# Weight conversion in the first chunk: steps of several pieces grouped by kind, and moved ahead of other work

## The chip, the cores and the metric

The kernel runs on one core of a Trainium2 chip. The core has a matrix engine (TensorE; PE in the profile), VectorE (DVE), ScalarE (ACT), GpSimd (POOL) and SyncE (SP), which here only issues transfers. Each engine works through its instructions in their order, and waits on semaphores for what others make. The metric is the device time of one execution in microseconds (us); less is better.

## The reference, cut to what matters

```python
# q, k, v, o_gate: (4, 8, 768, 40); i_gate, f_gate: (4, 8, 768)
for t in range(S):                                  # an mLSTM cell
    m_new = np.maximum(f_gate[:, :, t] + m, i_gate[:, :, t])
    f_stab = np.exp(f_gate[:, :, t] + m - m_new)
    i_stab = np.exp(i_gate[:, :, t] - m_new)
    C = f_stab * C + i_stab * einsum('bhd,bhe->bhde', vt, kt)
    n = f_stab * n + i_stab * kt
    y[:, :, t] = sigmoid(o_gate) * (C @ qt) / max(abs(n @ qt), 1)
x = y.transpose(0, 2, 1, 3).reshape(3072, 320)
h = x @ w_in                                        # w_in: (320, 2048)
out = (h * np.cos(h)) @ w_out                       # w_out: (2048, 320)
```

The two weights are float64 on the host: `randn(...)` times a float64 scale. They reach the chip as pairs of 32-bit words.

## The kernel before

The sequence is cut into 6 chunks of 128 steps; with 4 batches that makes 24 cells, numbered n = 4 c + b. The cells of chunk 0 are computed first, in a written order (`first_cells`). After that `both_parts(c, b)` (L956) does the feed-forward part of chunk c in two halves, f2 = 2b and 2b + 1, and along with it cell n = 4 (c + 1) + b of the next chunk. A half covers 256 of the 2048 columns of w_in. The change is in chunk c = 0 alone; "half 0" to "half 7" below are its f2 = 0 to 7, with cells 4 to 7.

The order of the program is the order on each engine (`tc.manual_schedule`). In a half come: `Up` (TensorE: w_in times x into two PSUM banks; L645 for the two 128-row parts, L639 for the last 64 rows, which come last in even halves and first in odd ones), `near` (ScalarE, L653), `rest` (VectorE, L656: the remainder), `sin` (ScalarE, L661) and `gate` (VectorE, L665), which frees the PSUM bank. There are two such banks, so `Up` of the next half waits for the gates of this one. `down_slot` multiplies what the half before gave with w_out (L677). In an even half the cell's scores (L479), their weighing (L485), its values (L505 to L514), `seam` (L597) and `normalize_turned` (from the transpose of the gate, oT, L457, to xT, L534) stand in between; in an odd half its state (L622), `weigh_k` of the next cell (GpSimd, kw, L407), the two transposes of its q and k (`turn_blocks`, VectorE, L452; the scores of the next half need them), and `scale_q` (GpSimd, qG, L461). `seam_out` in an odd half issues the transfer xL on ScalarE's queue.

**The conversion.** w_in comes in pieces `in f a`, `in f b` (128 rows by 512 columns each) and `in f c` (the last 64 rows, laid out as 128 by 256), f = 0 to 3; piece f holds the columns of halves 2f and 2f + 1. w_out comes in pieces `out0` to `out7` of 128 by 640; out p is used by `down` of half p. Each is brought as bits by SyncE (L139, four transfers of 128 KB for a and for b; L174, four of 64 KB for c; L180, one of 640 KB) and made float32 in six steps:

- `take_apart`: two on ScalarE, L150 (out of the high words) and L152 (low words, in place);
- `put_together`: a clamp (L157) and two shifts in one instruction (L159), both on VectorE with one input; a bitwise step on VectorE with two inputs (L161); an addition on GpSimd (L162).

The bits of w_in pieces lie in a ring of four buffers, those of w_out pieces in a ring of three. So the transfer of out p + 3 waits for the addition of out p, and on SyncE's queue everything behind it waits too. `next_out` (L952) converts the next w_out piece and issues the transfer of the one three later.

Before, in1a is converted in half 0, behind the cell's normalizing. Then:

| half | place: piece |
| --- | --- |
| 1 | before state and gates: in1b; after the gates: in1c; then SyncE: in2, q, k, v, E of cells 6 and 7; transposes, qG; out1, transfer of out4 |
| 2 | after the gates: in2a; out2, transfer of out5; behind normalizing: in2b |
| 3 | before state and gates: in2c; SyncE: in3, q, k, v, E, G of cells 8 and 9; transposes, qG; out3, transfer of out6 |
| 4 | after the gates: in3a; out4, transfer of out7; behind normalizing: in3b |
| 5 | before state and gates: in3c; transposes, qG; out5 |
| 6, 7 | after the gates: out6; after transposes and qG: out7 |

Of the kernel before, what the change touches and what calls it, by code (L numbers as in the profile page):

```python
# [11 lines left out]
FP = mybir.dt.float32  # L12
I32 = mybir.dt.int32
# [3 lines left out]
OP = mybir.AluOpType  # L17
# [12 lines left out]
def kernel(  # L30
# [20 lines left out]
    nc = tc.nc  # L51
# [87 lines left out]
            nc.sync.dma_start(out=bits[rows, 0:n], in_=piece)  # L139
        return bits  # L140

    def to_float32(dst, bits):
        take_apart(dst, bits)
        put_together(dst, bits)

    def take_apart(dst, bits):
        n = dst.shape[1]
# [3 lines left out]

        nc.scalar.activation(out=bits[:, 0:n, 0], in_=lo, func=AF.Copy, scale=2.0 ** -29)  # L152

    def put_together(dst, bits):
        n = dst.shape[1]
        hi, t, m = bits[:, 0:n, 1], dst.bitcast(I32), bits[:, 0:n, 0]
        nc.vector.tensor_scalar(out=t.bitcast(FP), in0=t.bitcast(FP), scalar1=LEAST, scalar2=GREATEST,  # L157
                                op0=OP.max, op1=OP.min)
        nc.vector.tensor_scalar(out=t, in0=t, scalar1=5, scalar2=2, op0=OP.logical_shift_left,  # L159
                                op1=OP.logical_shift_right)  # L160
        nc.vector.scalar_tensor_tensor(out=t, in0=hi, scalar=TOP2, in1=t, op0=OP.bitwise_and, op1=OP.bitwise_or)  # L161
        nc.gpsimd.tensor_tensor(out=t, in0=t, in1=m, op=OP.add)  # L162

# [665 lines left out]
    def first_cells():  # L829
        nc.vector.memset(nil, 0.0)  # L830
        gates_in()
        nc.scalar.copy(out=ident_b, in_=ident)
        load(0, "qk")
        later_gates_in()
        load(0, "v")
        load(1, "qk")
        load_o(0, (0, 1))
        load(1, "v")
        load(2, "qk")
        load_E(0)  # L840
# [60 lines left out]
        load_two(B, "Kv")  # L901
        load_E(B + 1)
        load_o(1)
        outs.append((0, weights_out(0)))
        weigh(2)
        decay_exponents(3)
        turn_out(3)
        seam_out(1)
        values(2)
        decay(3)  # L910
        weigh_k(3)
        state(1)
        normalize(2)
        scores(3)
        pg = gates_turn()
        warm(1)
        seam(2)
        weigh(3)
        to_float32(*pieces.pop(0))
        decay_exponents(B)  # L920
        pieces.extend(weights_in(1))
        outs.extend((p, weights_out(p)) for p in range(1, 3))
        seam_out(2)
        state(2)
        for piece in pieces[0:2]:
            take_apart(*piece)
        gates_keep(*pg)
        values(3)
        normalize(3)
        put_together(*pieces.pop(0))  # L930
        warm(3)
        seam(3)
        seam_out(3)
        put_together(*pieces.pop(0))
        low_dimensions(B)
        turn_blocks(B)
        state(3)
        load_E(B + 2)
        decay(B)
        sigmoid(1)  # L940
        weigh_k(B)
        odd_values(B)
        scale_q(B)
# [5 lines left out]

        nc.scalar.activation(out=spot, in_=spot, func=AF.Sin)  # L950

    def next_out():  # L952
        p, piece = outs.pop(0)
        to_float32(*piece)
        if p + 3 < NF // 2:
            outs.append((p + 3, weights_out(p + 3)))  # L956

    def both_parts(c, b):

        n = (c + 1) * B + b  # L960
        cell = n < N
        for i in range(2):
            f2 = 2 * b + i
            up = Up(c, f2)
            if cell and i == 0:
                scores(n)
                if c == 0 and b == 0:

                    warm(8, psum_o())
            if cell and i == 1:  # L970
                if n % 2 == 1 and n > B + 1 and n + 3 < N:
                    load_two(n + 3, "Kv")
            for e in range(2):
                up.near(e)
            for e in range(2):
                up.rest(e)
            if i == 0:
                if cell:
                    weigh(n)
                    if n + 1 < N:  # L980
                        decay_exponents(n + 1)
                    if n == B:
                        clear_low()
                for e in range(2):
                    up.sin(e)
                    up.gate(e)
                if c > 0:
                    sums(c, f2)
                if b == 0 and c == 1:
                    sigmoid(c + 1)  # L990

                if c == 0 and b > 0 and pieces:
                    to_float32(*pieces.pop(0))
                if c == 0:
                    next_out()
                if cell and n + 1 < N:
                    decay(n + 1)
            else:
                if cell:
                    seam_out(n)  # L1000
                if pieces:
                    to_float32(*pieces.pop(0))
                if cell:
                    state(n)
                for e in range(2):
                    up.sin(e)
                    up.gate(e)
                if c > 0:
                    sums(c, f2)
                if n == B + 1:  # L1010
                    low_dimensions(n + 1)
                while pieces:
                    to_float32(*pieces.pop(0))
                if cell and n + 1 < N:
                    weigh_k(n + 1)
                    odd_values(n + 1)
            if i == 1 and b == B - 1 and 0 < c < NC - 2:
                sigmoid(c + 2)
                sin_next()
            down_slot(c, f2)  # L1020
            if f2 == 0 and c > 1:
                for p in range(2):
                    combine_first(c - 1, p)
            if cell and i == 0:
                turn_gate(n)
                values(n)
                seam(n)
                normalize_turned(n)
                fade(n)
                if c == 1 and b < 3:  # L1030
                    weight_sums(b + 1)
                if n % 2 == 1 and n > B + 1 and n + 3 < N:
                    load_two(n + 3, "qk")
                if n > B + 1 and n + 3 < N:
                    load_E(n + 3)
                if b == B - 2 and c + 2 < NC:
                    load_o(c + 2)
                if c == 0 and pieces:
                    to_float32(*pieces.pop(0))
                sin_next()  # L1040
            if f2 == 0 and c > 1:
                for p in range(2):
                    combine(c - 1, p)
            if i == 1:
                if c == 0 and b + 2 < B:
                    pieces.extend(weights_in(b + 2))
                    load_two((n + 3) // 2 * 2)
                    load_E(n + 3)
                if cell and n + 1 < N:
                    turn_blocks(n + 1)  # L1050
                    scale_q(n + 1)
                if c == 0:
                    next_out()
                if (c, f2) == (0, LAST):
                    weight_sums(0)

    pieces, outs = [], []
# [41 lines left out]
```

## Time and profile before

| | us |
| --- | --- |
| median of 3 runs | 540.6 (539.52 to 541.74) |
| the profiled execution, its time | 540.66 |
| its span, first to last instruction | 538.9 |
| TensorE busy | 520.1 |
| VectorE busy | 421.9 |
| ScalarE busy | 285.7 |
| GpSimd busy | 224.7 |
| mean granted TensorE clock | 0.972 |

Half 1 begins at about 59 us, half 7 ends at about 140 us. How to read the profile's rows: in a timeline a row has the start in us, the duration, engine, line, operation, what is written and read, the count, and in brackets how long the engine stood idle before and what ended that. Matmuls of several instructions are merged into one row. A row of the chain has start, duration and what the end of the program waited for at that time; "DMA" is a transfer from its issue to its landing. "SPq" and "ACTq" are queues that issue transfers: their duration is that of issuing. A row of the waits has who waited for whom, the sum in us, the number and the longest. A row of one line has minimum, median and maximum duration in ns.

### The profile page before, as it was taken

Reading aid. Unit: us, or ns where it says so; the run is one execution under the profiler, and the core shown is the slowest. Engines: PE = TensorE matmul, PEld = TensorE weight load, DVE = VectorE, ACT = ScalarE, POOL = GpSimd, SP = SyncE. Lnnn points to the kernel's source line nnn. Section 1 sums busy time; section 2 is a strip of 40 time slices with the busy share of each in tenths; the row PEclk is TensorE's granted clock in tenths of the full one; section 3 lists DMA queues with packets and bytes.
Section 4 is the critical chain, followed back from the end, with each engine's and each line's share of the span. In section 5 each row is a group of like instructions: output and inputs, shape, how many; then the busy total and the mean of one; then the engine's idle time right before and its main releaser. Section 6 shows DMA issues by size and latency. Waiting matters only on the chain.

```text
span 538.9 us, 10497 instructions
## 1 busy us (share of the span) xinstructions
PE 520.1 (97%) x3844; PEld 353.7 (66%) x3844; DVE 421.9 (78%) x907; ACT 285.7 (53%) x546; POOL 224.7 (42%) x369
## 2 busy tenths in 40 slices
PE   7999879899999999999999999999999999999996
PEld 4885445545566767757767767767667767576755
DVE  5565889998788897898878898878898878663636
ACT  2587958666475446826527826526836522222221
POOL 7435454555477573533542632542421421221211
PEclk9587989999999999999999999999999999999999
DMA  9999884959847539329248329249220000000001
GB/s 137 220 213 233 248 169 142 213 92 253 176 116 171 67 94 191 42 93 202 28 120 174 43 88 193 35 125 174 40 79 7 2 5 6 19 33 1 0 1 49
DMA packets 99939, 57.81 MB, mean 107 GB/s; under 512 B 62304, under 2 KB 92608, under 8 KB 99888
## 3 DMA queue, kind: packets, MB, share of 16 engines
q1 hardware_dynamic: 96496, 55.64, 47.4%
q10 hardware_dynamic: 3248, 1.33, 1.2%
q8 instruction: 30, 0.49, 0.4%
q0 software_dynamic: 144, 0.18, 0.1%
q14 instruction: 21, 0.17, 0.1%
HBM read 51.71 MB, written 4.11 MB: 104 GB/s over the span
## 4 chain that ended last, share of the span: by engine, by line
PE 73%; DMA 9%; DVE 8%; SPq 4%; POOL 2%; ACT 1%; issue 1%; DVEq 0%; POOLq 0%
PE pup L645 26%; PE acc L755 24%; PE pup L639 8%; PE po L677 3%; PE late L755 3%; DMA bits<-in_moe_w_in_dram 3%; PE ps L479 3%; PE vt L514 2%; PE vt L505 2%; PE pu L597 1%; DMA E<-M_d 1%; DVE t L452 1%; DMA xL<-xT 1%; DMA bits<-in_moe_w_out_dram 1%; DMA G<-G_d 1%
## 5 line engine op out<-in xcount | busy, mean ns | idle before, releaser
L645 PE MATMUL pup<-xT,w_in_sb 128*128 128x512 f32 x384 | 177.8, 606 | 4.8 <-DVE g L665 4.5
L653 ACT ACTIVATE n<-pup 128x512 int32<-128x512 f32 x96 | 54.0, 595 | 195.3 <-PE pup L639 143.7
L645 PEld LDWEIGHTS pup<-xT,w_in_sb 128*128 128x128 f32 x384 | 70.6, 193 | 92.2 <-issue 87.9
L656 DVE SCALAR_TENSOR_TENSOR n<-pup,n 128x512 f32<-128x512 f32 x96 | 63.1, 687 | 76.3 <-ACT n L653 75.0
L719 POOL TENSOR_TENSOR D<-g 128x128 f32<-128x128 f32 x40 | 19.8, 495 | 218.6 <-DVE g L665 218.6
L661 ACT ACTIVATE n<-n 128x512 f32<-128x512 f32 x96 | 57.6, 627 | 21.8 <-DVE n L656 13.1
L665 DVE SCALAR_TENSOR_TENSOR g<-pup,n 128x512 f32<-128x512 f32 x96 | 61.7, 684 | 4.1 <-ACT n L661 3.5
L755 PE MATMUL acc<-w_out_sb,g 128*128 128x160 f32 x320 | 58.6, 304 | 0.0
L755 PE MATMUL acc<-T,g 128*128 128x160 f32 x320 | 58.0, 301 | 0.1
L639 PE MATMUL pup<-xL,w_in_l 64*128 64x512 f32 x192 | 54.2, 641 | 0.0
L755 PEld LDWEIGHTS acc<-w_out_sb,g 128*128 128x128 f32 x320 | 47.8, 190 | 5.6 <-issue 4.2
L755 PEld LDWEIGHTS acc<-T,g 128*128 128x128 f32 x320 | 48.1, 190 | 3.6 <-issue 2.9
L402 ACT ACTIVATE E<-E,tab 128x128 f32<-128x128 f32 x160 | 49.0, 388 | 0.3
L677 PE MATMUL po<-w_out_sb,g 128*128 128x320 f32 x128 | 36.2, 436 | 1.8 <-POOL w_out_sb L162 1.8
L755 PE MATMUL acc<-T,S 128*128 128x160 f32 x160 | 35.0, 301 | 0.0
L479 PEld LDWEIGHTS ps<-t,t 40*128 40x128 f32 x384 | 26.0, 196 | 11.3 <-issue 6.6
L677 PEld LDWEIGHTS po<-w_out_sb,g 128*128 128x128 f32 x128 | 24.1, 190 | 13.2 <-POOL w_out_sb L162 2.4
L485 DVE TENSOR_TENSOR E<-ps,E 128x512 f32<-128x512 f32 x48 | 30.7, 681 | 0.5 <-PE ps L479 0.5
L461 POOL TENSOR_TENSOR qG<-t,G 128x512 f32<-128x512 f32 x20 | 25.6, 1281 | 13.0 <-DVE t L452 6.5
L639 PEld LDWEIGHTS pup<-xL,w_in_l 64*128 64x128 f32 x192 | 14.5, 185 | 23.3 <-issue 19.0
L755 PE MATMUL acc<-w_out_sb,S 128*128 128x160 f32 x160 | 28.8, 299 | 0.0
L950 ACT ACT_TABLE_LOAD x22 | 28.2, 1283 | 0.4
(175 smaller groups left out, 883.5 us busy)
## 6 DMA issues: line engine op xcount, KB each, us to landing
E<-M_d SPq DMA_DIRECT2D x22, 512.0 KB
qr<-in_q_dram SPq DMA_DIRECT2D x36, 160.0 KB
kr<-in_k_dram SPq DMA_DIRECT2D x36, 160.0 KB
G<-G_d SPq DMA_DIRECT2D x20, 256.0 KB
bits<-in_moe_w_out_dram SPq DMA_DIRECT2D x8, 640.0 KB
bits<-in_moe_w_in_dram SPq DMA_DIRECT2D x32, 128.0 KB
out_dram<-o_sb SPq DMA_DIRECT2D x24, 160.0 KB
ks<-in_k_dram SPq DMA_DIRECT2D x10, 320.0 KB
```

The costliest lines, as they stand in the source:

```text
L402: nc.scalar.activation(out=Es[n][:, h], in_=Es[n][:, h], func=AF.Exp, scale=-1.0, bias=tab[:, c, 0, g:g + 1])
L479: nc.tensor.matmul(ps[j][:, p], kT[r, p], qT[r, p], start=True, stop=True)
L485: nc.vector.tensor_tensor(out=w, in0=pss[n][j], in1=w, op=OP.mult)
L639: nc.tensor.matmul(pu, w_in_l[r, f2], xL[c][r].rearrange("p b t -> p (b t)"), start=ahead, stop=not ahead)
L645: nc.tensor.matmul(pu.rearrange("p (b t) -> p b t", b=B), w_in_sb[:, i, ts(2 * f2 + e, 128)], xT[c][:, i:NK * B:NK], start=(i == 0 and not ...
L653: nc.scalar.activation(out=self.n[e], in_=self.pu[e], func=AF.Copy, bias=0.25)
L656: nc.vector.scalar_tensor_tensor(out=self.n[e].bitcast(FP), in0=self.pu[e], scalar=0.25, in1=self.n[e], op0=OP.add, op1=OP.subtract)
L661: nc.scalar.activation(out=r, in_=r, func=AF.Sin, scale=TWO_PI_DOWN)
L665: nc.vector.scalar_tensor_tensor(out=g, in0=self.pu[e], scalar=TWO_PI, in1=self.n[e].bitcast(FP), op0=OP.mult, op1=OP.mult)
L677: nc.tensor.matmul(po[c][b], gs[c, f][:, ts(b, C)], w_out_sb[:, f], start=(f == 0), stop=(f == NF - 1))
L755: nc.tensor.matmul(a, lhs, rhs, start=start, stop=stop)
L950: nc.scalar.activation(out=spot, in_=spot, func=AF.Sin)
```

## The change

`to_float32` takes several pieces: ScalarE's steps of all of them, then the clamps and shifts of all (`bound`, new), then the bitwise steps and additions of all. `next_out` takes the w_in pieces that are converted together with its own. In odd halves of chunk 0 all of them stand behind the gates and ahead of `down_slot`, the transfers of SyncE and the transposes. `weigh_k` goes behind `scale_q` in chunk 0. After it:

| half | place: pieces |
| --- | --- |
| 1 | after state and gates: in1b, in1c, out1 together, transfer of out4; then SyncE: in2, q, k, v, E; transposes, qG, kw |
| 2 | after the gates: in2a, out2 together, transfer of out5; behind normalizing: in2b |
| 3 | after state and gates: in2c, out3 together, transfer of out6; SyncE: in3, q, k, v, E, G; transposes, qG, kw |
| 4 | after the gates: in3a, out4 together, transfer of out7; behind normalizing: in3b |
| 5 | after state and gates: in3c, out5 together; transposes, qG, kw |
| 6, 7 | after the gates: out6; out7 |

In `first_cells` the order of instructions stays as it was.

```diff
-    def to_float32(dst, bits):
-        take_apart(dst, bits)
-        put_together(dst, bits)
+    def to_float32(*made):
+        for dst, bits in made:
+            take_apart(dst, bits)
+        for dst, bits in made:
+            bound(dst)
+        for dst, bits in made:
+            put_together(dst, bits)
...
+    def bound(dst):
+        t = dst.bitcast(I32)
+        nc.vector.tensor_scalar(out=dst, in0=dst, scalar1=LEAST, scalar2=GREATEST, op0=OP.max, op1=OP.min)
+        nc.vector.tensor_scalar(out=t, in0=t, scalar1=5, scalar2=2, op0=OP.logical_shift_left,
+                                op1=OP.logical_shift_right)
+
     def put_together(dst, bits):
         n = dst.shape[1]
         hi, t, m = bits[:, 0:n, 1], dst.bitcast(I32), bits[:, 0:n, 0]
-        nc.vector.tensor_scalar(out=t.bitcast(FP), in0=t.bitcast(FP), scalar1=LEAST, scalar2=GREATEST,
-                                op0=OP.max, op1=OP.min)
-        nc.vector.tensor_scalar(out=t, in0=t, scalar1=5, scalar2=2, op0=OP.logical_shift_left,
-                                op1=OP.logical_shift_right)
...
-    def next_out():
+    def next_out(*made):
         p, piece = outs.pop(0)
-        to_float32(*piece)
+        to_float32(*made, piece)
         if p + 3 < NF // 2:
             outs.append((p + 3, weights_out(p + 3)))
...
-                if c == 0 and b > 0 and pieces:
-                    to_float32(*pieces.pop(0))
                 if c == 0:
-                    next_out()
+                    next_out(*[pieces.pop(0) for _ in range(min(b, len(pieces), 1))])
...
                 if cell:
                     seam_out(n)
-                if pieces:
-                    to_float32(*pieces.pop(0))
                 if cell:
                     state(n)
...
                 if n == B + 1:
                     low_dimensions(n + 1)
-                while pieces:
-                    to_float32(*pieces.pop(0))
+                if c == 0:
+                    next_out(*pieces)
+                    pieces.clear()
                 if cell and n + 1 < N:
-                    weigh_k(n + 1)
+                    if c > 0:
+                        weigh_k(n + 1)
                     odd_values(n + 1)
...
                 if cell and n + 1 < N:
                     turn_blocks(n + 1)
                     scale_q(n + 1)
-                if c == 0:
-                    next_out()
+                    if c == 0:
+                        weigh_k(n + 1)
```

More of the change, by code (lines that the diff above doesn't have):

```diff
@@ L918, in first_cells @@
         weigh(3)
-        to_float32(*pieces.pop(0))
+        to_float32(pieces.pop(0))
         decay_exponents(B)
@@ L929, in first_cells @@
         normalize(3)
+        bound(pieces[0][0])
         put_together(*pieces.pop(0))
@@ L933, in first_cells @@
         seam_out(3)
+        bound(pieces[0][0])
         put_together(*pieces.pop(0))
@@ L1011, in both_parts @@
                     low_dimensions(n + 1)
-                while pieces:
-                    to_float32(*pieces.pop(0))
+                if c == 0:
+                    next_out(*pieces)
+                    pieces.clear()
                 if cell and n + 1 < N:
-                    weigh_k(n + 1)
+                    if c > 0:
+                        weigh_k(n + 1)
                     odd_values(n + 1)
@@ L1038, in both_parts @@
                 if c == 0 and pieces:
-                    to_float32(*pieces.pop(0))
+                    to_float32(pieces.pop(0))
                 sin_next()
```

## The prediction

> **What bounds the kernel now.** I read the page first, then the waits of TensorE, then the timelines of each engine from 60 to 145 us, then the chain over the same stretch. TensorE is busy 520.1 of 538.9 us. From 145 us on nothing that this change touches makes it wait, so what the first chunk gains or loses there goes to the end one for one.
>
> ```profile
> PE 520.1 (97%) x3844; PEld 353.7 (66%) x3844; DVE 421.9 (78%) x907; ACT 285.7 (53%) x546; POOL 224.7 (42%) x369
> PE pup L645 <- DVE g L665: 4.5, 3, 2.4
> PE po L677 <- POOL w_out_sb L162: 1.8, 3, 0.7
> 70.71 5.37 PE L645 MATMUL pup<-xT,w_in_sb 128*128 128x512 f32 x8 [2.41 <-DVE g L665]
> 95.40 3.67 PE L645 MATMUL pup<-xT,w_in_sb 128*128 128x512 f32 x8 [1.19 <-DVE g L665]
> 118.37 3.67 PE L645 MATMUL pup<-xT,w_in_sb 128*128 128x512 f32 x8 [0.94 <-DVE g L665]
> ...
> 74.45 1.44 DVE L159 TENSOR_SCALAR w_out_sb<-w_out_sb 128x640 int32<-128x640 int32 x1
> 83.50 1.48 DVE L159 TENSOR_SCALAR w_out_sb<-w_out_sb 128x640 int32<-128x640 int32 x1
> 83.20 1.43 POOL L162 TENSOR_TENSOR w_in_sb<-w_in_sb,bits 128x512 int32<-128x512 int32 x1 [3.72 <-ACT bits L152]
> ```
>
> Read there: TensorE waits three times for the gates of halves 1, 3 and 5 (2.41, 1.19, 0.94 us) and three times, 1.8 us together, for out1, out3 and out5. The second shift of a w_out piece lasts 0.49 us alone and 1.44 to 1.48 us when GpSimd adds at that moment. The second set of rows is SyncE's queue and the chain.
>
> ```profile
> 62.71 8.50 SPq L139 DMA_DIRECT2D bits<-in_moe_w_in_dram  x8
> 71.31 2.63 SPq L174 DMA_DIRECT2D bits<-in_moe_w_in_dram  x4
> ...
> 91.71 0.37 SPq L180 DMA_DIRECT2D bits<-in_moe_w_out_dram  x1
> 92.34 4.02 DMA bits<-in_moe_w_in_dram
> 97.10 4.56 DMA bits<-in_moe_w_in_dram
> 105.38 0.68 DVE w_in_sb L161
> 124.68 4.58 PE po L677 x16
> ...
> 398.57 0.58 DVE L714 TENSOR_TENSOR S<-g 128x128 f32<-128x128 f32 x1
> 398.55 0.46 POOL L719 TENSOR_TENSOR D<-g 128x128 f32<-128x128 f32 x1 [8.82 <-DVE g L665]
> 378.30 0.29 DVE L714 TENSOR_TENSOR S<-g 128x128 f32<-128x128 f32 x1
> L534 DVE TENSOR_TENSOR xT<-yt,db x20: 557/559/1010, 63.9 to 452.7; 128x384 f32<-128x384 f32 x20
> ```
>
> The pieces in2 are issued from 62.71 to 73.94, in3 from 92.34 to 99.32. Their use begins on ScalarE at 79.72 (in2a) and 102.71 (in3a).
>
> **What the change gains.** In halves 1, 3 and 5 one w_in conversion leaves the place ahead of the gates: in1b is 1.52 us of VectorE (67.46 to 68.98), in2c and in3c 1.25 each. Gates move up by as much, and so does TensorE's next Up, as far as the three waits go: at most 2.41 + 1.19 + 0.94 = 4.5 us. out1, out3, out5 come ahead of the two transposes: at most 1.8 us. The clamps and shifts no longer meet an addition: about 1 us of VectorE in each of halves 1, 2 and 4 and 0.7 in each of 3 and 5 (two clamps at 0.55 and 0.93 for 0.28 and 0.49); VectorE has no idle time from 100.85 to 122.9. After the 2.41 us hole the granted clock was 0.5 from 72.1 to 75.5, so another 1.7 us (5.37 less 3.67) could come back. The ceiling is 4.5 + 1.8 + 1.7 = 8.0 us.
>
> **What it costs, half by half.** All durations are start-to-start in the timelines: clamp and shift 0.45 + 0.46 us for in a/b, 0.32 + 0.33 for in c, 0.53 + 0.53 for out; bitwise steps (L161) 0.61, 0.34, 0.74; additions (L162) 1.28, 0.70, 1.55; ScalarE's two steps 0.58, 0.34, 0.69 each; 0.12 us from engine to engine.
>
> Half 1. State and gates now follow the remainders (67.5): 0.88 + 1.2 us, first gate done at 69.0, TensorE starts Up of half 2 at 69.1. But in1b and in1c are weights of this very Up. in1b's bitwise step now stands behind six clamps and shifts: 69.6 + 2.62 = 72.2, done at 72.85, its addition (which before ended at 70.5) at 74.4. TensorE has 1.82 us of work without it (to 70.95) and then waits 3.6 us. From 74.55: 1.82 + 1.06 + scores 0.9 = 78.35, or 80.05 if one stretch of 3.4 us falls to half clock as after the 2.41 us hole. Before, that point was 78.04, and the next matmuls began at 78.50. So half 1 gives back all it won: -0.15 to +1.5.
>
> SyncE. out4's transfer is now issued ahead of in2, q, k, v and E. It writes the buffer of out1, so it waits for out1's addition, and the whole queue with it. Additions: in1b 73.15 to 74.45, in1c, out1 to 77.45 (the order of steps is below). So in2 is issued from 77.5, not from 62.71. How long until in2a is there: from out5's issue at 91.71 the first slab of in3a landed at 96.36 (4.65 us, 0.79 MB) and the second slab of in3c, issued at 97.10, at 101.66 (9.95 us, 1.83 MB). Between them out plus a whole "a" piece (1.18 MB) takes 6.6 us; I take 6.5, with 4.3 (the first slab's own 4.02 and 0.3) and 7.4 (the chain's 5.36 us for out0 at 44.65, and four slabs at 0.5) as bounds. in2a lands at 84.0. ScalarE comes to it at 81.8 and waits; behind it stand out2's steps, the decay of the next cell and in2b; on VectorE the clamps wait, and normalizing the cell behind them. Clamps of in2a at 84.8, of out2 at 86.1, the oT transpose at 88.5 (before 85.76), remainders of half 3 at 94.1 (before 91.21), first gate of half 3 at 96.85, Up of half 4 at 97.0 against 95.40: the step won is spent, +1.5.
>
> Half 3. in2c's clamps wait for ScalarE, which copies q and k (1.68 us) first; out3's clamps go ahead of in2c's bitwise step; its addition ends at 102.0 where TensorE wants it at 100.6 (97.0 + 3.63): 1.5 us. Third set of matmuls of w_out at 104.3 against 101.72: +2.5.
>
> SyncE again. out6 goes ahead of in3 and waits for out3's addition, which ends at 103.6. in3a lands at 110.2, 7 us after ScalarE needed it before (102.71) and 4.5 after it is ready now. VectorE stands 3.3 us. oT at 114.6 (before 108.75), remainders of half 5 at 120.2 (114.18); the gates no longer wait for in3c: 122.3 (117.53); Up of half 6 at 123.1 (118.37); w_out's fifth set at 129.2 against 124.68: **+4.5**. From there TensorE runs on as before; in halves 6 and 7 out6 and out7 have 1.5 us and more of slack on VectorE (idle 1.68 at 135.94), and GpSimd's sums begin after out7 and qG as before.
>
> **Two-input steps beside additions.** The trace says what meets whom: L714 (both inputs in SBUF) lasts 0.29 us alone and 0.58 beside GpSimd's L719; L534 goes from 0.56 to 1.01 us. So in the groups a bitwise step and an addition take turns, and that is in the times above: out1's bitwise step waits for in1b's addition (0.85 to 1.3 us), in2c's and in3c's additions wait for out3's and out5's bitwise step (0.65). Without the taking of turns the same working ends at 2.6 instead of 4.5; I keep 4.5 because the rows show it. [...]
>
> On GpSimd out1's, out3's and out5's additions now stand ahead of qG, and kw behind it: qG of cell 5 runs from 77.5 to 78.7 and is wanted at 84.4, kw (1.0 us) later still; nothing, as long as w_out's matmuls (4.4 us) lie between.
>
> **Sum.** The profiled execution took 540.66 us with a span of 538.9, as good as the median 540.6. 540.66 + 4.5 = 545.2 us. With a landing in 4.3 us the same working gives +0.5 to +1.4, with 7.4 us +6.5 us.
>
> **Rivals.**
> 1. The transfers aren't late (in2 and in3 come by the time ScalarE asks): then only the hole of half 1 stays, and VectorE's saved stalls make up for it. The working with landing at once gives -0.7 (no fall of the clock) to +0.7: 540.7 us. For it: DMA stood idle from 87 to 91 us, so there was room. Against: that room lies before the additions that now release the queue.
> 2. Faster: VectorE is the bound of halves 3 to 5 (it is the chain from 105.38 on), and there its work ahead of the gates falls by 1.25 us, its stalls by 1.7 (halves 4 and 5) and as much one cell earlier. Then the four waits of those halves go, 1.19 + 0.70 + 0.94 + 0.68 = 3.5 us, with half 1 even: 537.2. It decides if in2a is there by 81.8 and in3a by 103, and if the scores needn't wait for the transposes, which now stand behind a whole group. Against: in3 can't leave before out3's addition, and 103 less 6.5 is 96.5, when in2c's clamps have just begun.
> 3. Worse: SyncE's later transfers also wait for the xL transfer of the half, as at 91.71 (idle since 81.4, released as xL landed), now with q and k of cell 6 behind it: ScalarE's copies in half 3 come 2 to 3 us later, and with them out3, out6 and in3: 547.9.
>
> **Chances.** Forecast 0.52, first rival 0.22, second 0.09, third 0.17. The forecast's own range by the landing's bounds is 541.5 to 547.2. Within 0.5% (2.7 us, so 538.0 to 543.4) a measurement of this kernel can hardly tell a change from none. Of the forecast's 0.52, 0.04 falls in there, and of the first rival's 0.22, 0.02 lies below: same 0.20 + 0.04, faster 0.09 + 0.02, slower 0.48 + 0.17. The range 539.5 to 548.5 takes in the first rival and most of the third, and leaves out the second and the far end of the third.
>
> **What would show it.** In the profile after: a wait of TensorE in L645 for POOL's w_in addition of about 3.6 us near 71; SyncE's w_out issue at about 77.5 ahead of eight w_in issues, not 62.7; ScalarE waiting in L150 for the w_in transfer in halves 2 and 4 (2 and 4.5 us); L159 never above 0.6 us; fewer or no waits of L677 for L162. I am wrong if in3a's ScalarE step starts by 104, or if L645's waits for gates are gone and nothing stands in their place.

## The result, and the profile after

| | before | after |
| --- | --- | --- |
| median on the same chip | 540.99 us (538.37 to 541.74, 8 runs) | 543.21 us (542.13 to 545.33, 8 runs) |
| ratio, 95% interval | | 1.0057 (1.0031 to 1.0083) |
| profiled execution's span | 538.9 us | 541.8 us |
| mean granted TensorE clock in it | 0.972 | 0.980 |
| TensorE busy | 520.1 us | 518.0 us |

By the means the change makes the kernel 0.57% slower, some 3.1 us; the medians differ by 2.2 us. TensorE works no longer than before; it stands idle longer. The line numbers have moved: Up is L651 and L645 (before L645 and L639), down L683 (L677), ScalarE's first conversion step L154 (L150), clamp and shift L160 and L161, bitwise step L167, addition L168, the w_out transfer L186, the gates L671. In what follows "down5" is the set of w_out matmuls that stands in half 6, with what half 5 gave, and so on.

First TensorE's timeline of the kernel after; the brackets hold the idle time and what ended it.

```profile
72.63 3.49 PE L651 MATMUL pup<-xT,w_in_sb 128*128 128x512 f32 x4 [2.48 <-POOL w_in_sb L168]
95.26 3.67 PE L651 MATMUL pup<-xT,w_in_sb 128*128 128x512 f32 x8 [1.19 <-DVE g L671]
100.21 1.13 PE L645 MATMUL pup<-xL,w_in_l 64*128 64x512 f32 x4 [1.28 <-POOL w_in_l L168]
115.55 4.57 PE L683 MATMUL po<-w_out_sb,g 128*128 128x320 f32 x16 [1.47 <-POOL w_out_sb L168]
121.47 3.67 PE L651 MATMUL pup<-xT,w_in_sb 128*128 128x512 f32 x8 [1.34 <-DVE g L671]
127.55 4.57 PE L683 MATMUL po<-w_out_sb,g 128*128 128x320 f32 x16
```

The 2.41 us for the gates of half 1 are gone, and 2.48 us for in1b's addition stand in their place. The waits for gates in halves 3 and 5 (before 1.19 and 0.94 us) are still there, though no w_in piece stands ahead of the gates any more: the whole half comes later. down5 begins at 127.55, before at 124.68.

Why it comes later is in the timelines of SyncE's queue, ScalarE and VectorE.

```profile
61.28 14.49 SPq L186 DMA_DIRECT2D bits<-in_moe_w_out_dram  x2
75.83 4.38 SPq L139 DMA_DIRECT2D bits<-in_moe_w_in_dram  x8
90.51 11.57 SPq L186 DMA_DIRECT2D bits<-in_moe_w_out_dram  x2
102.13 4.20 SPq L139 DMA_DIRECT2D bits<-in_moe_w_in_dram  x8
82.37 0.68 ACT L154 ACTIVATE w_in_sb<-bits 128x512 f32<-128x512 f32 x1 [2.37 <-DMA bits<-in_moe_w_in_dram]
108.50 0.68 ACT L154 ACTIVATE w_in_sb<-bits 128x512 f32<-128x512 f32 x1 [4.49 <-DMA bits<-in_moe_w_in_dram]
109.22 0.43 DVE L160 TENSOR_SCALAR w_in_sb<-w_in_sb 128x512 f32<-128x512 f32 x1 [3.48 <-ACT w_in_sb L154]
```

The first row joins the issue of out3's transfer with that of out4's; in between SyncE's queue stands until out1's addition lets go of the buffer (the addition ends at 75.38, the issue at 75.77). The third is the same with out5, out6 and out3's addition. in2 is issued from 75.83 instead of 62.71, in3 from 102.13 instead of 92.34. ScalarE then waits 2.37 us for in2a and 4.49 us for in3a, 6.54 and 6.37 us after the issue, and VectorE stands 3.48 us behind it. The table of waits has a row that the one before lacked:

```profile
ACT w_in_sb L154 <- DMA bits<-in_moe_w_in_dram: 6.9, 2, 4.5
```

The chain tells less here: it runs over two of in3's transfers after the change (issued at 102.13 and 107.31) as it did before (92.34 and 97.10).

### The profile page after: what moved, and what is told of

The parts are those of the page before. It is cut to its first block, busy times and chain, and to the rows that moved or that the text cites. A ratio compares the mean times of both kernels' runs of the same rounds, so it can differ in the third digit from the quotient of the medians.

```text
span 541.8 us, 10496 instructions
## 1 busy us (share of the span) xinstructions
PE 518.0 (96%) x3844; PEld 349.5 (65%) x3844; DVE 420.1 (78%) x907; ACT 285.1 (53%) x546; POOL 227.0 (42%) x369
## 4 chain that ended last, share of the span: by engine, by line
PE 75%; DVE 9%; DMA 7%; POOL 2%; SPq 2%; ACT 2%; issue 2%; DVEq 0%; POOLq 0%; ACTq 0%
PE pup L651 27%; PE acc L761 23%; PE pup L645 8%; PE po L683 3%; PE ps L485 3%; PE late L761 3%; DMA E<-M_d 2%; PE vt L520 2%; DMA bits<-in_moe_w_in_dram 2%; PE vt L511 2%; DMA xL<-xT 1%; PE pu L603 1%; DVE g L671 1%; DMA vs<-in_v_dram 1%; SPq L330 1%
## 5 line engine op out<-in xcount | busy, mean ns | idle before, releaser
L651 PE MATMUL pup<-xT,w_in_sb 128*128 128x512 f32 x384 | 178.4, 607 | 5.2 <-DVE g L671 2.5
L651 PEld LDWEIGHTS pup<-xT,w_in_sb 128*128 128x128 f32 x384 | 70.3, 192 | 93.0 <-issue 88.1
L671 DVE SCALAR_TENSOR_TENSOR g<-pup,n 128x512 f32<-128x512 f32 x96 | 61.6, 683 | 3.9 <-ACT n L667 3.3
L645 PE MATMUL pup<-xL,w_in_l 64*128 64x512 f32 x192 | 54.3, 642 | 1.3 <-POOL w_in_l L168 1.3
L683 PE MATMUL po<-w_out_sb,g 128*128 128x320 f32 x128 | 36.4, 437 | 1.5 <-POOL w_out_sb L168 1.5
L485 PEld LDWEIGHTS ps<-t,t 40*128 40x128 f32 x384 | 24.6, 188 | 12.5 <-DVE t L458 6.6
L683 PEld LDWEIGHTS po<-w_out_sb,g 128*128 128x128 f32 x128 | 23.8, 190 | 13.4 <-POOL w_out_sb L168 3.1
L645 PEld LDWEIGHTS pup<-xL,w_in_l 64*128 64x128 f32 x192 | 14.6, 186 | 25.1 <-issue 19.8
L761 PEld LDWEIGHTS acc<-T,S 128*128 128x128 f32 x160 | 26.2, 190 | 3.0 <-issue 3.0
```

Of the source, the lines that this page charges most:

```text
L485: nc.tensor.matmul(ps[j][:, p], kT[r, p], qT[r, p], start=True, stop=True)
L645: nc.tensor.matmul(pu, w_in_l[r, f2], xL[c][r].rearrange("p b t -> p (b t)"), start=ahead, stop=not ahead)
L651: nc.tensor.matmul(pu.rearrange("p (b t) -> p b t", b=B), w_in_sb[:, i, ts(2 * f2 + e, 128)], xT[c][:, i:NK * B:NK], start=(i == 0 and not ...
L671: nc.vector.scalar_tensor_tensor(out=g, in0=self.pu[e], scalar=TWO_PI, in1=self.n[e].bitcast(FP), op0=OP.mult, op1=OP.mult)
L683: nc.tensor.matmul(po[c][b], gs[c, f][:, ts(b, C)], w_out_sb[:, f], start=(f == 0), stop=(f == NF - 1))
L761: nc.tensor.matmul(a, lhs, rhs, start=start, stop=stop)
```

## The experiments

**The yardstick.** The first cells end at another time in each run, so the runs are compared over one stretch as well: from the first rest of half 1 on VectorE to the first matmul of down5. It is 58.43 us before (66.25 to 124.68) and 62.69 after (64.86 to 127.55). Times are medians, and each ratio is to runs of the kernel before on the same chip; those had medians of 539.1 to 541.0 us, so the ratios compare, and not the times.

| kernel | to down1 | to down3 | yardstick, to down5 | time, us | ratio to before (95%) |
| --- | --- | --- | --- | --- | --- |
| before | 12.25 | 35.47 | 58.43 | 540.99 | |
| before once more | 12.28 | 36.27 | 59.21 | 539.01 (one run) | |
| after | 13.28 | 37.82 | 62.69 | 543.21 | 1.0057 (1.0031 to 1.0083) |
| after once more | 11.64 | 37.87 | 62.59 | 542.05 | 1.0059 (1.0029 to 1.0089) |
| after, transfers late | 11.64 | 34.35 | 55.37 | 536.37 | 0.9946 (0.9919 to 0.9973) |
| after, out4 early, out6 late | 13.28 | 37.97 | 58.99 | 538.89 | 1.0005 (0.9981 to 1.0029) |
| after, one by one | 12.52 | 39.02 | 64.78 | 545.11 | 1.0117 (1.0079 to 1.0156) |
| before, SyncE's order changed | 12.27 | 41.05 | 68.63 | 548.34 | 1.0178 (1.0141 to 1.0216) |
| late, one by one | 12.23 | 36.28 | 58.19 | 539.05 | 0.9994 (0.9967 to 1.0022) |
| late, gates behind | 11.49 | 33.53 | 55.58 | 534.12 | 0.9913 (0.9881 to 0.9944) |
| late, out behind turning | 12.72 | 36.37 | 58.82 | 542.48 | 1.0042 (1.0015 to 1.0069) |
| late, in1b first | 11.57 | 33.78 | 54.80 | 534.61 | 0.9925 (0.9895 to 0.9954) |
| before, out ahead alone | 11.36 | 33.41 | 56.32 | 536.18 | 0.9950 (0.9927 to 0.9972) |
| the best halves together | 10.55 | 32.57 | 53.59 | 533.67 | 0.9903 (0.9875 to 0.9931) |

Two profiles of the kernel before differ by 0.78 us in the yardstick, two of the kernel after by 0.10. Differences below about 1 us are not read from it. In the profile before the granted clock was 0.50 from 72.11 to 75.52 us, and the eight matmuls from 70.71 took 5.37 us for 3.67; sets of other runs that take as much longer (1.65 to 1.70 us) are called a stretch at half clock too.

### What repeats

The changed kernel and the kernel before, unchanged.

> The changed kernel once more, to learn what repeats. Yardstick for all runs: from the first rest of half 1 on VectorE to the first matmul of down5 (before 66.25 to 124.68 = 58.43 us, after 64.86 to 127.55 = 62.69 us). Theory (the late transfers cost it, wherever the first cells end): 62.3 to 63.1 again, holes ahead of Up in half 1 near 2.5 and ahead of out3's down near 1.5, time 1.003 to 1.008 of before. Rival (the place where the first cells end decides as much as the change): the yardstick moves by over 1 us with the start of half 1.

> The kernel before once more, to learn what of its profile repeats. In the profile before, half 1 starts at 66.25 us at a mean granted clock of 0.972; in all later profiles it starts between 63.14 and 64.93 at 0.977 to 0.987. Theory (the start is set by the half-speed stretches of the first cells, which differ from run to run): yardstick 58.0 to 58.8 us wherever half 1 starts, and a start near 63.5 if the granted clock is 0.985. Rival (before starts half 1 late by its program): start 66 +- 0.5 at any clock.

The loss repeats: 62.59 us and a ratio of 1.0059. The hole of half 1 is 2.88 us, behind another of 0.90 for the gates, and down2 waits 1.63 us for out2's addition; the hole that the expectation calls out3's is that of down4, for out4's addition, 1.44 us. The kernel before now starts half 1 at 63.31 us with a granted clock of 0.981, so the late start at 66.25 belonged to that execution. Its yardstick, 59.21, is 0.4 above what was expected.

### The transfers late

```diff
         to_float32(*made, piece)
-        if p + 3 < NF // 2:
-            outs.append((p + 3, weights_out(p + 3)))
+        return p + 3
+
+    def fetch_out(p):
+        if p < NF // 2:
+            outs.append((p, weights_out(p)))
...
-                    next_out(*pieces)
+                    later = next_out(*pieces)
                     pieces.clear()
...
                     if c == 0:
                         weigh_k(n + 1)
+                if c == 0:
+                    fetch_out(later)
```

In even halves the transfer stays right behind the conversion.

> After, with the transfers of out4 and out6 issued at the end of their halves as in before, behind in2/in3, q, k, v and E; all conversions stay where after has them. Theory (SyncE's order is the cause): in2a and in3a land as early as in before, ScalarE's waits for them (2.37 and 4.49 us) go, the yardstick is 57.5 to 59.9 us (the hole of half 1 stays near 2.5) and the time 540.0 to 541.7. Rival (the places and grouping of the conversions are the cause): the yardstick stays at 61.5 us or more and the time at 542.5 or more.

SyncE's queue, ScalarE's waits and TensorE in half 1 of this kernel, from the timelines:

```profile
60.17 11.46 SPq L139 DMA_DIRECT2D bits<-in_moe_w_in_dram  x8
82.08 7.10 SPq L186 DMA_DIRECT2D bits<-in_moe_w_out_dram  x2
89.32 3.81 SPq L139 DMA_DIRECT2D bits<-in_moe_w_in_dram  x8
71.49 1.98 PE L651 MATMUL pup<-xT,w_in_sb 128*128 128x512 f32 x4 [2.88 <-POOL w_in_sb L168]
119.08 4.58 PE L683 MATMUL po<-w_out_sb,g 128*128 128x320 f32 x16
```

in2 and in3 are issued from 60.17 and 89.32 and ScalarE doesn't wait for them. The yardstick falls by 7.2 us, from 62.59 to 55.37, and the time to 0.9946 of before. That is further than the theory said: without the late transfers the rest of the change is a gain of about 3 us, not nothing. The hole of half 1 stayed at 2.88 us, so it was not what made the kernel slower.

### One of the two transfers

```diff
                     later = next_out(*pieces)
                     pieces.clear()
+                    if b == 0:
+                        fetch_out(later)
...
-                if c == 0:
+                if c == 0 and b > 0:
                     fetch_out(later)
```

> The version with late transfers, but out4's transfer issued where after issues it, ahead of in2, q, k, v and E; out6's stays late. From half 1's first rest to down3 after took 37.87 us and the version with late transfers 34.35. Theory (each of the two transfers adds its own loss, nothing is caught up): 37.5 to 38.2 to down3, 58.4 to 59.3 to down5, time 539 to 540.5. Rival (what out4 costs is caught up in halves 4 and 5 if in3 isn't late as well): 37.5 to 38.2 to down3, but 55.4 to 57.5 to down5, time 536 to 538.

```profile
59.55 14.30 SPq L186 DMA_DIRECT2D bits<-in_moe_w_out_dram  x2
73.90 4.50 SPq L139 DMA_DIRECT2D bits<-in_moe_w_in_dram  x8
88.35 0.39 SPq L186 DMA_DIRECT2D bits<-in_moe_w_out_dram  x1
94.17 5.09 SPq L139 DMA_DIRECT2D bits<-in_moe_w_in_dram  x8
```

out4's issue again holds the queue for 14.30 us (first row), while the next w_out row is out5's issue alone, 0.39 us. down3 comes at 37.97 us, 3.62 later than with both transfers late, and down5 3.62 later too (58.99 against 55.37): nothing is caught up. The second transfer adds 62.59 - 58.99 = 3.60 us. Each of the two costs 3.6 us of the yardstick, and by the ratios (0.9946, 1.0005, 1.0059) 3.2 and 2.9 us of the time. This run has a stretch at half clock in half 1, 1.65 us (2.88 us for 1.98 and 1.88 for 1.13, at 70.70 and 73.51), which the version with late transfers lacks; it isn't what is lost, since of the two profiles of the kernel after one has such a stretch and one has none, and they reach down3 at 37.82 and 37.87.

### SyncE's order alone

The kernel before, with the transfers of in2 and in3 and of the next cells' q, k, v and E behind that of out4 and out6; no engine but SyncE gets another order.

```diff
-                if c == 0 and b + 2 < B:
-                    pieces.extend(weights_in(b + 2))
-                    load_two((n + 3) // 2 * 2)
-                    load_E(n + 3)
                 if cell and n + 1 < N:
                     turn_blocks(n + 1)
                     scale_q(n + 1)
                 if c == 0:
                     next_out()
+                if c == 0 and b + 2 < B:
+                    pieces.extend(weights_in(b + 2))
+                    load_two((n + 3) // 2 * 2)
+                    load_E(n + 3)
```

> Before, with SyncE's order alone changed: at the end of halves 1 and 3 the transfers of in2/in3, q, k, v and E come behind the transfer of out4/out6, which waits for out1's/out3's addition (ends 78.44 and 101.67 in before). Theory: in2 is issued from 78.9 instead of 62.7, in2a lands near 85.3 and in3a near 109 (used at 79.7 and 102.7 in before): yardstick 63 to 65.5 us, time 545 to 548. Rival (the transfers are hidden wherever they stand): yardstick 58.4, time 540 to 541.5.

```profile
82.74 0.70 ACT L150 ACTIVATE w_in_sb<-bits 128x512 f32<-128x512 f32 x1 [6.74 <-DMA bits<-in_moe_w_in_dram]
111.32 0.67 ACT L150 ACTIVATE w_in_sb<-bits 128x512 f32<-128x512 f32 x1 [4.82 <-DMA bits<-in_moe_w_in_dram]
...
75.88 6.26 PE L677 MATMUL po<-w_out_sb,g 128*128 128x320 f32 x16 [2.19 <-POOL w_out_sb L162]
97.41 5.37 PE L645 MATMUL pup<-xT,w_in_sb 128*128 128x512 f32 x8 [3.22 <-DVE g L665]
118.17 6.22 PE L677 MATMUL po<-w_out_sb,g 128*128 128x320 f32 x16 [2.11 <-POOL w_out_sb L162]
```

The order of one queue is enough: 68.63 us and 1.78% slower. It is more than was expected: in this execution three holes (2.19, 3.22, 2.11 us) were each followed by matmuls at half clock, 6.26, 5.37 and 6.22 us for sets that take 4.57, 3.67 and 4.57 at full clock. The kernel before has one such stretch in each of its profiles; the two more, 3.4 us, are about as much as the run lies above the expected range (3.1).

### The group

In both versions, with the transfers of after and with the late ones, each piece's clamp, shift, bitwise step and addition are issued before the next piece's.

```diff
         for dst, bits in made:
             take_apart(dst, bits)
-        for dst, bits in made:
             bound(dst)
-        for dst, bits in made:
             put_together(dst, bits)
```

> After, with the pieces of a group converted one after the other, clamp, shift and bitwise step together, everything else as in after. Theory (SyncE's order is the cause): in1b's bitwise step comes 1.7 us earlier (0.32 + 0.33 + 0.53 + 0.53), the hole ahead of Up in half 1 falls from 2.5 to about 0.8 us, but out1's addition, and so out4's transfer, comes no earlier: yardstick 62 to 63 us, time 542.5 to 543.5. Rival (the grouping is the cause): yardstick 58.5 to 60, time 540 to 541.5.

> The version with late transfers, its pieces converted one after the other instead of as a group. Yardstick (first rest of half 1 to down5): 55.37 us with the group, 58.43 before. Theory (the group is a gain of its own: in the run one by one with the transfers of after, the yardstick was 64.78 against 62.59): 57 to 58.5 us, time 538 to 540. Rival (the group costs half 1's hole of 2.88 and the loss of that other run came only through the transfers): 54.5 to 55.5 us, time 535 to 536.5.

Both come out slower than with the group, by 2.2 and 2.8 us of the yardstick. So the first expectation missed on both sides: in1b's hole fell, to 0.44 us, as the theory had it, but VectorE lost more than that. Two rows of VectorE's timeline and two of TensorE's, pieces one by one with late transfers:

```profile
68.78 1.32 DVE L159 TENSOR_SCALAR w_in_l<-w_in_l 128x256 int32<-128x256 int32 x1
80.41 1.46 DVE L159 TENSOR_SCALAR w_out_sb<-w_out_sb 128x640 int32<-128x640 int32 x1
...
74.78 1.16 PE L483 MATMUL ps<-t,t 40*128 40x128 f32 x16 [1.73 <-DVE t L456]
75.87 6.27 PE L681 MATMUL po<-w_out_sb,g 128*128 128x320 f32 x16
```

And VectorE and GpSimd with the group, late transfers:

```profile
68.14 0.29 DVE L161 TENSOR_SCALAR w_in_l<-w_in_l 128x256 int32<-128x256 int32 x1
70.21 1.91 DVE L167 SCALAR_TENSOR_TENSOR w_out_sb<-bits,w_out_sb 128x640 int32<-128x640 int32 x1
80.16 0.49 DVE L161 TENSOR_SCALAR w_out_sb<-w_out_sb 128x640 int32<-128x640 int32 x1
...
81.40 1.75 POOL L168 TENSOR_TENSOR w_in_sb<-w_in_sb,bits 128x512 int32<-128x512 int32 x1 [3.88 <-issue]
```

One by one, a shift beside an addition takes 1.32 us instead of 0.29 (in1b's addition, 68.68 to 69.95), or 1.46 instead of 0.49 (in2a's, 80.11 to 81.52). In the group these stalls are gone, but the two-input step takes 1.91 us (0.83 one by one) and in2a's addition 1.75 (1.41 one by one). From in1b's clamp to the end of out1's bitwise step the group takes 5.10 us (67.02 to 72.12), one by one 5.84 (66.94 to 72.78); in half 2, 3.14 against 4.36. The transposes come that much earlier: with the group scores waited 0.23 us in half 4 and nowhere else up to 140 us, one by one 1.73 in half 2, 1.07 in half 4 and 0.62 in half 6. With late transfers, 1.7 of the 2.8 us are a stretch at half clock that only the run one by one has, behind the scores' wait of 1.73 us (6.27 us for down1, 4.57 with the group); about 1.1 are left. With the transfers of after the 2.2 us can't be split so: that run has such a stretch too, but so has one of the two profiles of after, and their yardsticks are the same (62.69 and 62.59).

### Gates, and w_out's second piece

From the version with late transfers, one edit undone at a time. First in1b, in2c and in3c ahead of the gates again:

```diff
                     seam_out(n)
+                if pieces:
+                    to_float32(pieces.pop(0))
                 if cell:
                     state(n)
```

> The version with late transfers, with in1b, in2c and in3c converted ahead of the gates of halves 1, 3 and 5 as in before; in1c, out1, out3 and out5 stay behind the gates. Theory (gates first only exchanges one wait for another: half 1 waits 0.89 + 2.88 for 2.41, half 3 1.11 + 0.23 for 1.19, half 5 nothing for 0.94): yardstick 54.5 to 56.5 us, time 535 to 537.5. Rival (gates first is the gain of the version with late transfers): 57.5 to 58.5 us, time 538.5 to 540.

Then out1, out3, out5 and out7 behind the transposes and qG again:

```diff
-                    later = next_out(*pieces)
+                    to_float32(*pieces)
                     pieces.clear()
...
                 if c == 0:
-                    fetch_out(later)
+                    fetch_out(next_out())
```

> The version with late transfers, with out1, out3, out5 and out7 converted behind the transposes and their copies, as in before. Theory (w_out's second piece ahead of turning is worth TensorE's three waits for it, 0.46 + 0.70 + 0.68): yardstick 56.6 to 57.3 us, time 537.5 to 539. Rival (it is worth nothing, as the additions would come in time): 55.0 to 55.8 us, time 536 to 537.

With the w_in pieces ahead of the gates nothing is lost: 55.58 us against 55.37, and a ratio of 0.9913, whose interval meets that of 0.9946. TensorE then waits 1.02, 0.32 and 0.79 us for the gates of halves 1, 3 and 5; with the gates first it waited 0.89 us for gates and 2.88 for in1b in half 1, and 1.11 for in2c in half 3. Gates first exchanges one wait for another, and may lose by it: the run with w_in ahead is 1.8 us the faster by the ratios, and its yardstick holds about 0.9 us in which VectorE waited in half 1, where TensorE was only 0.1 us ahead of it. That it loses is not shown. w_out's second piece is another matter. TensorE's rows with out1, out3 and out5 behind the transposes:

```profile
75.86 4.58 PE L683 MATMUL po<-w_out_sb,g 128*128 128x320 f32 x16 [1.94 <-POOL w_out_sb L168]
...
99.51 4.57 PE L683 MATMUL po<-w_out_sb,g 128*128 128x320 f32 x16 [2.55 <-POOL w_out_sb L168]
...
121.96 4.57 PE L683 MATMUL po<-w_out_sb,g 128*128 128x320 f32 x16 [1.35 <-POOL w_out_sb L168]
```

5.8 us of waits for w_out, where the kernel before had 1.8: with gates and w_in faster, TensorE comes to these matmuls sooner and finds w_out not ready. It costs 3.45 us of the yardstick, more than expected. The time, 542.48 us, is 6.1 above that of the version with late transfers; the profiled execution (539.11 us) was the shortest of the twelve, and what the longer ones lost was not profiled.

The same part by itself: the version with late transfers, with the edit of the first (w_in ahead of the gates) and with the pieces one by one. Against the kernel before, the place of w_out's second piece, and with it of `weigh_k` behind `scale_q`, is all that differs (cut to the lines that do it):

```diff
-                while pieces:
-                    to_float32(*pieces.pop(0))
+                if c == 0:
+                    later = next_out(*pieces)
+                    pieces.clear()
                 if cell and n + 1 < N:
-                    weigh_k(n + 1)
+                    if c > 0:
+                        weigh_k(n + 1)
...
                     scale_q(n + 1)
+                    if c == 0:
+                        weigh_k(n + 1)
                 if c == 0:
-                    next_out()
+                    fetch_out(later)
```

> One part of the change alone: out1, out3, out5 and out7 are converted ahead of turning (and weigh_k behind it); their transfers stay at the end of the halves, w_in pieces ahead of the gates, and every piece is converted alone, as in before. Theory (this part is the gain: undoing it in the version with late transfers cost 3.45 us): yardstick 55.0 to 56.0 us, time 535 to 537. Rival (it gains only with the pieces in a group, which alone cost 2.8 us to undo): 57 to 58.5 us, time 538 to 540.

56.32 us lies between the two expectations. The part alone is worth 2.1 to 2.9 us of the yardstick, and 0.5% of the time (0.9927 to 0.9972). Of this, 1.7 us lie in the stretch at half clock behind a hole of 2.41 or 2.19 us that both profiles of the kernel before have and this run has not. With the group, otherwise the same, it is 55.58 us and 0.9913; this 0.7 us is less than the yardstick tells, and the intervals of the two ratios meet.

### The hole of half 1, and the best halves

Late transfers, in1b converted alone behind the gates, then in1c and out1 as a group:

```diff
                 if c == 0:
+                    if b == 0:
+                        to_float32(pieces.pop(0))
                     later = next_out(*pieces)
```

> The version with late transfers, with in1b converted alone behind the gates of half 1 and in1c and out1 as a group after it. Theory (in1b's bitwise step stood behind four one-input steps more, 1.7 us): the hole of 2.88 us falls to 1.2 or less, down1 comes 1.0 to 1.7 us earlier, yardstick 53.7 to 54.5 us, time 535 to 536. Rival (the clamps and shifts of in1c and out1 then meet in1b's addition, so out1 and in1c are later by as much): hole 1.2, but yardstick 55 to 56 us, time 536 to 537.

And the version in which in1b and in2c come ahead of the gates, in3c in a group behind:

```diff
                     seam_out(n)
+                if pieces and b < 2:
+                    to_float32(pieces.pop(0))
                 if cell:
                     state(n)
```

> The best halves together: late transfers, pieces in groups, in1b and in2c converted ahead of the gates of halves 1 and 3, in3c in a group behind the gates of half 5. Theory (halves add up: 11.49 + 22.04 + 11.24 + 9.78): yardstick 54.3 to 54.9 us, time 533 to 534.5. Rival (a gain in one half is lost in the next): 55.3 to 55.8 us, time 534 to 535.5.

The first missed its mechanism: the hole fell from 2.88 to 1.48 us, but now in1c's addition was late by 0.76 and down1 came only 0.07 us earlier; 0.5 of the yardstick's 0.57 us came in half 3. The second is the fastest version run: 533.67 us, 0.97% below before (0.69% to 1.25%), TensorE waiting for these pieces no more:

```profile
68.72 3.67 PE L651 MATMUL pup<-xT,w_in_sb 128*128 128x512 f32 x8 [1.29 <-DVE g L671]
73.72 1.16 PE L485 MATMUL ps<-t,t 40*128 40x128 f32 x16 [0.23 <-DVE t L458]
90.77 3.67 PE L651 MATMUL pup<-xT,w_in_sb 128*128 128x512 f32 x8 [0.25 <-DVE g L671]
95.73 1.16 PE L485 MATMUL ps<-t,t 40*128 40x128 f32 x16 [0.24 <-DVE t L458]
117.85 4.58 PE L683 MATMUL po<-w_out_sb,g 128*128 128x320 f32 x16
```

These are all of TensorE's waits from 60 to 140 us, 2.0 us in sum, and the start of down5. The yardstick fell by more than the halves add up to (53.59, expected 54.3 to 54.9); TensorE stood 1.3 us ahead of VectorE when half 1 began here and 0.1 in the run that half 1's term came from, which the yardstick doesn't see.

**Put in a row**, the parts are, in us of the yardstick: kernel before 58.4 to 59.2; w_out's second piece ahead, 56.3; pieces in groups, 55.6; gates first, 55.4; out4's transfer with it, 59.0; out6's too, 62.6. The ratios in the same order are 1, 0.9950, 0.9913, 0.9946, 1.0005 and 1.0059. Three edits win about 3.4 us, of which only the first one's part is clear of the noise, and what came along on SyncE's queue loses 7.2 us of the yardstick and about 6 of the time.

Not tried: a fourth buffer for w_out, with which out4 needn't wait for out1's addition. That the wait, and not the mere place of 640 KB ahead of w_in, does the harm is seen in the kernel before: there out5's transfer is issued at 91.71, right ahead of in3 at 92.34, and ScalarE takes in3a up at 102.71 without a wait.

## Why the prediction was right, and where not

The direction and the mechanism were right, and the sum for the loss nearly so; the price of the first rival, the case without late transfers, was wrong.

- **Half 1.** Predicted: the wait for the gates goes, a wait of 3.6 us for in1b's addition comes, net -0.15 to +1.5. Measured: 2.48 and 2.88 us, down1 at 13.28 and 11.64 us against 12.25 and 12.28, so +1.0 and -0.6: the first with a stretch at half clock behind the hole, the second without, as the two ends of that sum had it, each some 0.5 us below. In the profile after, VectorE began half 1 1.4 us earlier than in the one before and TensorE did not, which takes as much off the hole. In the second, both began about 2 us earlier, and the waits for the gates and for in1b come to 0.90 + 2.88 = 3.8 us.
- **SyncE and out4.** Predicted: in2 issued from 77.5, landing 6.5 us later, in2a at 84.0. Measured: 75.83, 6.54, 82.37: 1.6 us earlier, most of it the 1.4 us by which half 1 began earlier.
- **Half 3.** Predicted: in2c's addition 1.5 us late, down3 +2.5. Measured: 1.28 us, and 37.82 against 35.47, +2.35.
- **out6.** Predicted: in3a 4.5 us after it is wanted, VectorE standing 3.3, down5 +4.5. Measured: 4.49, 3.48, and down5 at 62.69 against 58.43, +4.26 (+3.4 against the second profile of before).
- **The signs.** The second shift lasts at most 0.50 us after the change, as said, and in3a's step starts at 108.50, beyond the 104 that would have refuted the sum. Not as said: the waits for w_out's additions are fewer (one, and two in the second profile, for three) but not shorter, 1.5 and 3.1 us against 1.8 and 3.6.
- **Steps that take turns.** The rows are there: out1's bitwise step 1.90 us for 0.83, in2a's addition 1.75 for 1.43, in2c's 1.19 for 0.74. They show steps that last longer beside each other (out1's bitwise step from 71.36 to 73.26, in1b's and in1c's additions from 71.24 to 73.85); that one waits for the other was the prediction's reading. No run took this away, so the 1.9 us that the prediction hung on it are not shown by themselves. The long shifts of w_out pieces (1.44 and 1.48 us, at most 0.50 after) are gone, and two-input steps are the long ones now. Against the pieces one by one, with late transfers, this is a gain, 0.74 us of VectorE in half 1 and 1.22 in half 2. One reading was off: the long shift at 74.45 in the kernel before met GpSimd's qG (73.98 to 75.53), not an addition.
- **The size.** 545.2 was predicted, 543.2 measured; +4.5 us against 0.57% and 0.59%, 3.1 and 3.2 us. The term that was too large is the +4.5 for down5, by 0.2 to 1.1 us, as the yardstick has it. Behind down5 nothing is lost or won: from there to the end every profile takes 414.2 us, but for before once more (414.7) and out behind turning (415.4), which bears out that the first chunk's loss goes to the end one for one. So what remains lies ahead of half 1: in the profile after it began 1.39 us earlier than in the one before, and 4.26 less 1.39 is the 2.9 us between the two spans. How much of that is the execution (below) and how much the kernel, two profiles of each don't settle.
- **The rivals: the step that failed.** "The working with landing at once gives -0.7 (no fall of the clock) to +0.7: 540.7 us" for the first rival. The version with late transfers is that case, and took 0.9946 of before, 2.9 us less. The second rival had the price (537.2 us, 3.5 us less) and the condition: in2a there by 81.8 and in3a by 103. With late transfers ScalarE waits for neither, VectorE begins their clamps at 78.85 and 101.05 (half 1 began 2.5 us earlier here), and the four waits that it priced (1.19, 0.70, 0.94, 0.68) are gone, with 1.11 us for in2c's addition and 0.23 for the scores in place of the first two. The two rivals described one case at two prices, and the larger chance went to the wrong one. Most of what the first left out is half 5: there the group's saved stalls and the gates together remove every wait, 9.78 us from down4 to down5 for 11.72; one by one it is 10.67, with w_in ahead of the gates 10.81.
- **Third rival.** out6's transfer was not held beyond out3's addition; its issue ended at 102.08, as that addition (100.11 + 1.57) let it go. It didn't happen.

## What to carry to other kernels

When a conversion moves, ask what else its helper issues: here the move of w_out's second pieces was worth 2 to 3 us, and the two refills that came with it, waiting for its buffer at the head of a queue that also brings the next weights, cost about 6. A transfer that has to wait for a buffer belongs behind those that needn't. Price the case in which your main mechanism fails as carefully as the main case: it tells what a small repair would bring.

## What the hardware showed unexpectedly

The time of this kernel's runs goes with the granted TensorE clock. Among the runs of the kernel before, those at a mean granted clock of 0.987 took 535.8 to 537.8 us, those at 0.972 541.0 to 541.6; those at 0.980 to 0.982, in between, took anything from 536.9 to 541.5. Most of the time at half speed lies in the first cells, in other places in the profile before than in that after, each stretch a multiple of 3.41 us long: 13.65 us (14.08 to 27.74) and 10.24 (37.98 to 48.22) before, where half 1 starts at 66.25, and 13.65 (32.00 to 45.66) and 3.41 (55.90 to 59.31) after, where it starts at 64.86. Nor does a hole decide by its length whether the clock falls. Two rows of the kernel before once more, and then two of the kernel after once more, both TensorE's timeline:

```profile
67.77 3.67 PE L645 MATMUL pup<-xT,w_in_sb 128*128 128x512 f32 x8 [2.43 <-DVE g L665]
75.59 6.26 PE L677 MATMUL po<-w_out_sb,g 128*128 128x320 f32 x16 [2.19 <-POOL w_out_sb L162]
```

```profile
72.12 1.98 PE L651 MATMUL pup<-xT,w_in_sb 128*128 128x512 f32 x4 [2.88 <-POOL w_in_sb L168]
75.98 4.57 PE L683 MATMUL po<-w_out_sb,g 128*128 128x320 f32 x16
```

Behind holes of 2.43 and 2.19 us the set of sixteen took 6.26 us, behind one of 2.88 it took 4.57. Between 62 and 125 us the fourteen profiles together have nine stretches at half clock: behind holes of 1.73 us in the two runs one by one, and of 2.11 to 3.22 us in the others. Behind others of 2.42 (before, SyncE's order changed), 2.55 (late, out behind turning) and 2.88 us (after, transfers late) the sets took their usual time: 3.67, 4.57, and 1.98, 1.13 and 4.57 us.

What decides was not shown. The profiles before and after give one more measure. Counted in steps of 3.41 us from the changes of the clock, TensorE was busy for 0.41 of the step just ahead of the fall in the one (68.70 to 72.11) and for 0.28 in the other (69.55 to 72.96); no other step between 62 and 125 us had less than 0.57, and the clock stayed at 1.00 behind each. So where a hole lies may count beside its length; two falls don't settle it.
